# A list scheduler with other hand-over times and another choice, and some weight tiles placed 64 bytes in

## The chip, the cores and the metric

The kernel runs on one core of a Trainium2 chip. The metric is the device time of one launch in microseconds (us), the median over several runs.

## The reference

Three blocks follow one another: a retention (attention with decay and without softmax), a mixture of eight experts, and a feed-forward network with a squared ReLU.

```
def _attn_ref(q, k, v):                      # 8 x 8 heads, 576 positions, 64 wide
    scores = scale * np.matmul(q, k.transpose(0, 1, 3, 2))
    Dmat = np.where(rel >= 0, gamma[:, None, None] ** rel[None, :, :], 0.0)
    return np.matmul(scores * Dmat[None, :, :, :], v)

def _moe_ref(x, modality_id, w_gate, modality_bias, w1, w2):   # x: 4608 x 512, w1: 8 x 512 x 1024
    e_idx = np.argmax(x @ w_gate + modality_bias[modality_id], axis=1)
    ...
        h = np.maximum(x[mask] @ w1[e], 0.0)
        out[mask] = gate_w[mask, None] * (h @ w2[e])

def _moe2_ref(x, w_in, w_out):               # w_in: 512 x 2048, w_out: 2048 x 512
    h = np.maximum(x @ w_in, 0.0)
    return h * h @ w_out
```

All is float32. The kernel gets that accuracy from TensorE by splitting each operand into a high and a low part (type fp32r in the profile) and adding three products: high by high, high by low, low by high.

## The kernel before

The program has three stages, one after the other on every engine. Up to 182 us it computes the retention and the gate. Up to 609.7 us it runs the experts: tokens are sorted into slots (a first one called E, then 0 to 8), each of which is one tile of tokens for one expert. A slot is 512 tokens wide, but slots 6, 7 and 8 are narrow: 448, 384 and 256. In `first` and `second` (matmuls in lines 839 to 841) TensorE holds a 128 x 128 block of the expert's weights, `wx` or `wy`, and streams the tokens, `xh`/`xl` or `hh`/`hl`, past it. `wsplit` writes `wx` and `wy` (high and low parts) into buffers of the pool `wp`. Beside the experts this stage prepares the weights of the feed-forward network in memory (`wc`).

The rest, to the end, is the feed-forward network in `phase3`, on which most of the change bears. It is done by a scheme of seven products in place of eight for 2 x 2 blocks. The tokens are nine tiles of 512, and the hidden width is worked off in three passes of 3, 2 and 3 blocks (`q`), so there are 27 steps `n` of one pass and one tile; pass 1 takes the tiles in reverse. A **group** is six matmuls of TensorE, 128 x 256 each (lines 1211 to 1213). `one(n, q, x)` records one group for product x of the first layer, in the order x = 1, 2, 6, 5, 7, 4, 3, into a bank X, Y or Z, and what follows it: copies of a bank to a tile `z` by ScalarE (line 1186), additions by VectorE (line 1189, an operand from a bank), squares (`sq`: line 1197 on VectorE, or lines 1194 and 1195 on ScalarE), and the splits of `z` into the high part of `h` (ScalarE, line 1320) and the low part (VectorE, line 1321). `two(n, x)` records the groups of the second layer, one for each q, into a bank R, and the additions of the result to `oe` or, in every second tile, to the same place in `yr`. There are two banks for X, two for Y, one for Z, so a group waits until the copy or addition of an earlier product has read its bank.

In pass 0, `xprep` makes the seven operands of the next tile from the tokens in `yr`: eight additions in place and seven pairs of a copy (high part) and a subtraction (low part), into the tiles `x0` to `x3`; `xc` keeps them for the later passes, which load them. In the last pass the rows of a finished tile go out by four scatters, issued by GpSimd (line 1328).

`Plan` holds all that `phase3` records, with a duration for each entry. `emit` gives each entry a due time (its place in the recorded order of TensorE, less the durations and hand-overs behind it, with a `SLACK` for work on the other engines) and then places entries one at a time: those whose inputs are placed are candidates, each with the earliest start on its engine. The order so chosen is fixed; at run time engines only wait for one another's semaphores. So the numbers in `Plan` set nothing but the order of each engine's instructions, and for `sq` also the engine.

Of the kernel before, what the change touches and what calls it, by code (L numbers as in the profile page):

```python
# [10 lines left out]
F32R = mybir.dt.float32r  # L11
# [11 lines left out]
NT, DM = B * S, H * D  # L23
NE, FE = 8, 1024
FF = 2048
P = 128
NTILE = NT // P
TS = 512
# [4 lines left out]
KD = DM // P  # L33
# [59 lines left out]
def kernel(ctx, tc, qT, kT, kN, vN, modT, w_gate, mbias, w1, w2, w_in, w_out,  # L93
# [6 lines left out]
    wp = ctx.enter_context(tc.tile_pool(name="wp", bufs=10))  # L100
# [326 lines left out]
    def new(pool_, shape, dt, tag, name):  # L427
        return fixed[name] if name in fixed else pool_.tile(shape, dt, tag=tag, name=name)
# [15 lines left out]
    def expert(s):  # L444
        src = eslot[0:1, 0:1] if s == "E" else slots[0:1, 0, s:s + 1]
        ereg.clear()
        ereg[s] = sp.value_load(src, min_val=0, max_val=NE - 1)

    def wsplit(key, h, eng):
        if h == 0:  # L450
            x = new(wp, [P, 2, KD, 2 * P], F32R, "w", "wx")
            split(x[:, 0], x[:, 1], raws.pop((key, 0)), eng)
            W[key] = [x]
        else:
            y = new(wp, [P, 2, 2, DM], F32R, "w", "wy")
            split(y[:, 0], y[:, 1], raws.pop((key, 1)), eng)
            W[key].append(y)

# [2 lines left out]
    def width(s):  # L461
        return WIDE.get(s, TS)
# [252 lines left out]
    def phase12():  # L715
        ring[0] = psG
        with ExitStack() as c1:
# [258 lines left out]
            def extras():  # L976
                fixed.update({
                    "wr1": wr.tile([P, KD, 2 * P], F32, tag="wr", name="cwr1"),
                    "wr2": wr.tile([P, 2, DM], F32, tag="wr", name="cwr2"),
                    "wx": wp.tile([P, 2, KD, 2 * P], F32R, tag="w", name="cwx"),  # L980
                    "wy": wp.tile([P, 2, 2, DM], F32R, tag="w", name="cwy"),
                    "ix": ip.tile([P, 4], I32, tag="ix", name="cix"),
                    "xg": rp.tile([P, 4, DM], F32, tag="raw", name="cxg"),
                    "xh": xp.tile([P, KD, TS], F32R, tag="xh", name="cxh"),
                    "xl": xp.tile([P, KD, TS], F32R, tag="xl", name="cxl"),
                    "pst": psG.tile([P, 4, P], F32, tag="g", name="cpst"),
                    "psh": psG.tile([P, TS], F32, tag="g", name="cpsh"),
                    "hh": hp.tile([P, TS], F32R, tag="hh", name="chh"),
                    "hl": hp.tile([P, TS], F32R, tag="hl", name="chl"),
                })  # L990
                fixed["ye"] = fixed["xg"]
                fixed["y0"] = fixed["y2"] = tpb
                fixed["y1"] = fixed["y3"] = psG.tile([P, TS], F32, tag="g", name="cyb")
                extra(0)
                fixed.clear()
# [7 lines left out]
            for i, u in enumerate(us):  # L1003
                s, f = u
                k = seq.index(s)
# [83 lines left out]
    AT1 = {1: 0, 2: 1, 6: 3, 5: 5, 7: 6, 4: 9, 3: 11}  # L1089

    class Plan:
        HAND = 0.25
        SLACK = 6.0
        OVER = {"ACT": 0.14, "DVE": 0.11}

        def __init__(self):
            self.ops, self.wrote, self.read = [], {}, {}

        def add(self, engs, fn, r=(), w=(), land=0.0):
            deps = set()  # L1100
# [10 lines left out]
                self.wrote[k] = [i]  # L1111
                self.read[k] = []

        def emit(self, ahead=400, near=0.15):
            n = len(self.ops)
            lat = lambda i: min(t for _, t in self.ops[i][0])
            at, due = 0.0, [0.0] * n
            for i, (engs, _, _, _) in enumerate(self.ops):
                due[i] = at + (0.0 if engs[0][0].name == "PE" else self.SLACK)
                at += engs[0][1] if engs[0][0].name == "PE" else 0.0  # L1120
            for i in range(n - 1, -1, -1):
                engs, _, deps, _ = self.ops[i]
                for d in deps:
                    same = len(engs) == 1 and self.ops[d][0] and self.ops[d][0][0][0] is engs[0][0]
                    due[d] = min(due[d], due[i] - lat(d) - self.ops[d][3] - (0.0 if same else self.HAND))
            free, end, on, starts = {}, {}, {}, []
            todo = list(range(n))
            ready = {}
            while todo:
                cand = []  # L1130
                for i in todo[:ahead]:
                    engs, fn, deps, land = self.ops[i]
                    if i not in ready:
                        if any(d not in end for d in deps):
                            continue
                        ready[i] = [max([end[d] + (0 if on[d] == e.name else self.HAND) for d in deps],
                                        default=0.0) for e, _ in engs]
                    _, s0, e, t = min(((max(r_, free.get(e.name, 0.0)) + t, max(r_, free.get(e.name, 0.0)), e, t)
                                       for (e, t), r_ in zip(engs, ready[i])), key=lambda z: z[:2])
                    cand.append((s0, due[i], i, e, t))  # L1140
                first_ = min(c[0] for c in cand)
                lead = min((c for c in cand if c[0] == first_), key=lambda c: c[1:3])
                s0, _, i, e, t = min((c for c in cand if c[0] <= first_ + near and c[3] is lead[3]),
                                     key=lambda c: c[1:3])
                free[e.name] = s0 + t * (1.0 - self.OVER.get(e.name, 0.0))
                end[i] = s0 + t + self.ops[i][3]
                on[i] = e.name
                starts.append((s0, len(starts), i, e))
                todo.remove(i)
            for s0, _, i, e in sorted(starts, key=lambda z: z[:2]):  # L1150
                self.ops[i][1](e.h)
            self.starts = starts
# [5 lines left out]
    def phase3():  # L1158
        with ExitStack() as c2:
            ff = c2.enter_context(tc.tile_pool(name="ff", bufs=1))  # L1160
            sb = lambda name, shape, dt=F32R: ff.tile(shape, dt, tag=name, name=name)
            plan = Plan()
            for j in (1, 2):
                wload2(1, j, wp, False)
            WT = [[[held["w", m, j, x] for x in range(2)] for j in range(3)] for m in range(2)]
            XT = [held["x", m] for m in range(7)]
            HT = [sb(f"h{j}", [P, 2 * 7 * 256 + 128])[:, 56 + 32 * (j % 2):56 + 32 * (j % 2) + 2 * 7 * 256]
                  .rearrange("p (x m c) -> p x m c", x=2, m=7) for j in range(3)]
            ZT = [sb(f"z{j}", [P, 8, 256], F32) for j in range(3)]
            yr = rp.tile([P, KD, TS], F32, tag="raw", name="yr")  # L1170
# [7 lines left out]
            PE_, ACT_, DVE_, POOL_, DMA_ = (Eng(n_, h_) for n_, h_ in  # L1178
                                            (("PE", pe), ("ACT", act), ("DVE", dve), ("POOL", pool), ("DMA", sp)))
# [33 lines left out]
                        e.matmul(ps[n], ll, rh, start=False, stop=True, skip_group_check=True)  # L1213
                return go

            MMS = [(PE_, 0.72)]

            def loadw(p, m, j0=0):
                for j, fp in list(enumerate(PASSES[p]))[j0:]:
# [50 lines left out]
            def one(n, q, x):  # L1270
# [6 lines left out]
                kx, ky, kz = ("X", u % 2), ("Y", u % 2), ("Z",)  # L1277
                z, h = ZT[u % 3], HT[u % 3]
                kz_ = lambda *i: [("z", u % 3, j) for j in i]
# [52 lines left out]
            def two(n, x):  # L1332
# [4 lines left out]
                for q in range(len(PASSES[p])):  # L1337
                    u = HS_[n, q]
                    h, m, w, mo = HT[u % 3], MH[x], WT[1][q], MO[x]
                    plan.add(MMS, six([ps[:, 0, :], ps[:, 1, :]],  # L1340
                                      [((h[:, 0, m, P * b:P * b + P], h[:, 1, m, P * b:P * b + P]),
# [108 lines left out]
```

## Time and profile before

| | us |
|---|---|
| median of 3 runs (1332.58 to 1333.44) | 1332.95 |
| the profiled execution, its own time | 1330.45 |
| its span in the trace | 1328.7 |

The profiled execution's span lies 1.75 us inside its own time, and that time lies 2.5 us under the median. TensorE's granted clock is at its full level (1.00) in nearly all of the span. An engine can be called busy and still lose time: a matmul's end is modelled, so a wait is best read from the distance between the starts of two matmuls.

### The profile page before, as it was taken

The page shows a single profiled execution, that of the slowest core. Times are in us where ns is not written, and L with a number is a line of the kernel's source. Part 1 is how long each engine was busy: PE and PEld are TensorE (multiplying, and loading weights), DVE is VectorE, ACT ScalarE, POOL GpSimd, SP SyncE. Part 2 cuts the span into 40 slices and gives each one's busy share as a digit, 9 for nine tenths or more (in the row PEclk, how much of TensorE's full clock was granted, in tenths as well). Part 3 has the DMA queues.
Part 4 walks back from the last instruction along what each step waited for, and adds up shares of the span by engine and source line. Part 5 has one row for each costly group of instructions (what it writes and reads, how often), then busy time and mean ns, then how long its engine had stood idle before and what let it go on. Part 6 is the DMA issues. An engine that isn't in the chain of part 4 may idle for free.

```text
span 1328.7 us, 26978 instructions
## 1 busy us (share of the span) xinstructions
PE 1284.4 (97%) x10639; PEld 1196.3 (90%) x10639; DVE 1023.2 (77%) x2095; ACT 623.1 (47%) x1283; POOL 125.3 (9%) x170
## 2 busy tenths in 40 slices
PE   7999989999999999899999999999999999999996
PEld 6888877888888888899999999999999999999996
DVE  3877859878887887665888888867888777777665
ACT  2344444545445444454655556534344344443343
POOL 3222112101100110000000000000000011111121
PEclk9999999999999999899999999999999999999999
DMA  9998257787777877779555554678799866555451
GB/s 330 390 346 300 88 183 245 264 296 272 279 280 264 285 258 270 273 268 351 206 205 221 219 197 175 245 263 309 289 348 345 298 225 211 206 196 175 175 192 47
DMA packets 152499, 331.89 MB, mean 250 GB/s; under 512 B 15440, under 2 KB 67440, under 8 KB 152368
## 3 DMA queue, kind: packets, MB, share of 16 engines
q1 hardware_dynamic: 144752, 309.82, 65.5%
q0 software_dynamic: 5840, 19.14, 4.0%
q8 instruction: 85, 1.39, 0.4%
q10 hardware_dynamic: 1776, 1.17, 0.3%
q14 instruction: 46, 0.38, 0.1%
HBM read 222.33 MB, written 107.78 MB: 248 GB/s over the span
## 4 chain that ended last, share of the span: by engine, by line
PE 40%; DVE 12%; DMA 1%; issue 1%; ACT 0%; POOL 0%; POOLq 0%; DVEq 0%
PE bank L1213 13%; PE bank L1211 13%; PE bank L1212 13%; DVE z L1189 5%; DVE h L1321 3%; DVE z L1197 2%; DMA x<-xc 1%; DVE x L1189 1%; DVE yr L1189 1%; PE bank L839 0%; PE bank L840 0%; PE bank L841 0%; ACT h L1320 0%; DVE oe L1189 0%; POOL out L1328 0%
## 5 line engine op out<-in xcount | busy, mean ns | idle before, releaser
L1211 PE MATMUL bank<-x,w 128*128 128x256 f32 x1008 | 279.6, 277 | 7.5 <-ACT z L1186 5.4
L1212 PE MATMUL bank<-x,w 128*128 128x256 f32 x1008 | 279.4, 277 | 4.4 <-DVE x L1189 4.4
L1211 PE MATMUL bank<-w,h 128*128 128x256 f32 x1008 | 279.9, 278 | 2.6 <-DVE oe L1189 2.0
L1213 PE MATMUL bank<-w,h 128*128 128x256 f32 x1008 | 279.6, 277 | 0.7 <-DVE h L1321 0.7
L1213 PE MATMUL bank<-x,w 128*128 128x256 f32 x1008 | 278.6, 276 | 0.0
L1212 PE MATMUL bank<-w,h 128*128 128x256 f32 x1008 | 278.4, 276 | 0.0
L1186 ACT ACTIVATE z<-bank 128x256 f32<-128x256 f32 x288 | 108.4, 380 | 231.6 <-PE bank L1213 229.9
L1320 ACT ACTIVATE h<-z 128x512 fp32r<-128x512 f32 (+2 forms) x270 | 158.5, 600 | 89.8 <-DVE z L1189 71.1
L1211 PEld LDWEIGHTS bank<-x,w 128*128 128x128 f32 x1008 | 189.3, 188 | 9.4 <-ACT z L1186 6.9
L1212 PEld LDWEIGHTS bank<-x,w 128*128 128x128 f32 x1008 | 189.2, 188 | 6.0 <-DVE x L1189 6.0
L1211 PEld LDWEIGHTS bank<-w,h 128*128 128x128 f32 x1008 | 189.3, 188 | 3.9 <-DVE oe L1189 2.6
L1213 PEld LDWEIGHTS bank<-w,h 128*128 128x128 f32 x1008 | 189.2, 188 | 1.5 <-DVE h L1321 1.4
L1213 PEld LDWEIGHTS bank<-x,w 128*128 128x128 f32 x1008 | 189.3, 188 | 0.1
L1212 PEld LDWEIGHTS bank<-w,h 128*128 128x128 f32 x1008 | 189.3, 188 | 0.0
L1321 DVE TENSOR_TENSOR h<-z,h 128x512 fp32r<-128x512 f32 (+2 forms) x270 | 169.1, 649 | 7.6 <-ACT h L1320 7.6
L1189 DVE TENSOR_TENSOR z<-z,bank 128x256 f32<-128x256 f32 x216 | 89.4, 417 | 64.0 <-PE bank L1213 55.2
L839 PE MATMUL bank<-xh,wx 128*128 128x512 f32 (+3 forms) x320 | 119.5, 373 | 4.1 <-ACT xh L794 2.7
L839 PE MATMUL bank<-hh,wy 128*128 128x512 f32 (+3 forms) x320 | 122.7, 383 | 0.0
L840 PE MATMUL bank<-xl,wx 128*128 128x512 f32 (+3 forms) x320 | 119.2, 373 | 1.0 <-DVE xl L795 1.0
L840 PE MATMUL bank<-hl,wy 128*128 128x512 f32 (+3 forms) x320 | 119.8, 374 | 0.2 <-DVE hl L856 0.2
L841 PE MATMUL bank<-hh,wy 128*128 128x512 f32 (+3 forms) x320 | 119.7, 374 | 0.0
L841 PE MATMUL bank<-xh,wx 128*128 128x512 f32 (+3 forms) x320 | 119.1, 372 | 0.0
(185 smaller groups left out, 2131.0 us busy)
## 6 DMA issues: line engine op xcount, KB each, us to landing
x<-xc SPq DMA_DIRECT2D x112, 512.0 KB
wr<-w SPq DMA_DIRECT2D x80, 512.0 KB
xc<-x SPq DMA_DIRECT2D x63, 512.0 KB
wc<-cwh SPq DMA_DIRECT2D x16, 896.0 KB
wc<-cwl SPq DMA_DIRECT2D x16, 896.0 KB
w<-wc SPq DMA_DIRECT2D x16, 896.0 KB
pd<-oe SPq DMA_DIRECT2D x24, 512.0 KB
xd<-xs SPq DMA_DIRECT2D x9, 1024.0 KB
```

What stands on the lines that cost most here:

```text
L839: pe.matmul(ps, lh, rh, start=first, stop=False)
L840: pe.matmul(ps, lh, rl, start=False, stop=False)
L841: pe.matmul(ps, ll, rh, start=False, stop=last)
L1186: plan.add(a_(c), lambda e: e.activation(o, i, f), r, w)
L1189: plan.add(engs or d_(c), lambda e: e.tensor_tensor(out=o, in0=a, in1=b, op=op), r, w)
L1197: e.scalar_tensor_tensor(out=z, in0=z, scalar=0.0, in1=z, op0=ALU.max, op1=ALU.mult)
L1211: e.matmul(ps[n], lh, rh, start=first and n == 0, stop=False, skip_group_check=True)
L1212: e.matmul(ps[n], lh, rl, start=False, stop=False, skip_group_check=True)
L1213: e.matmul(ps[n], ll, rh, start=False, stop=True, skip_group_check=True)
L1320: plan.add(a_(c), lambda e: e.activation(h[:, 0, a:b], z[:, a + 1:b + 1], AF.Copy), rs, ks[0])
L1321: plan.add(d_(c), lambda e: e.tensor_tensor(out=h[:, 1, a:b], in0=z[:, a + 1:b + 1], in1=h[:, 0, a:b].bitcast(F32), op=ALU.subtract), rs + ...
```

## The change

Four things are edited. (1) In `Plan` one hand-over time between engines, 0.25, becomes three: from TensorE 0.20, to TensorE 0.10, between the others 0.05; a group is put at 0.685 in place of 0.72, `SLACK` is 10 in place of 6. (2) In `emit` the choice among the candidates: before, the engine of the earliest candidate was taken and on it, of those that could start within 0.15, the one that was due first; now simply the candidate that can start first, and of equals the one that is due first. (3) In `wsplit` (and the tiles that stand in for it in the extra slots, `cwx` and `cwy`) the buffers are 64 elements longer, and the weights of slots 6, 7 and 8 begin 16 elements, 64 bytes, in. (4) The tiles `HT` are 64 elements shorter and begin at 56, 24 and 56 elements, in place of 56, 88 and 56.

```
+    def place(key, t):
+        o = 0 if width(key[0]) == TS else 16
+        return t[:, o:o + 8 * 2 * P]
+
     def wsplit(key, h, eng):
         if h == 0:
-            x = new(wp, [P, 2, KD, 2 * P], F32R, "w", "wx")
+            x = place(key, new(wp, [P, 2 * KD * 2 * P + 64], F32R, "w", "wx")).rearrange(
+                "p (x k f) -> p x k f", x=2, k=KD)
...
     class Plan:
-        HAND = 0.25
-        SLACK = 6.0
+        FROM_PE, TO_PE, HAND = 0.20, 0.10, 0.05
+        SLACK = 10.0
...
+        def hand(self, a, b):
+            if a == b:
+                return 0.0
+            return self.TO_PE if b == "PE" else self.FROM_PE if a == "PE" else self.HAND
...
-                first_ = min(c[0] for c in cand)
-                lead = min((c for c in cand if c[0] == first_), key=lambda c: c[1:3])
-                s0, _, i, e, t = min((c for c in cand if c[0] <= first_ + near and c[3] is lead[3]),
-                                     key=lambda c: c[1:3])
+                s0, _, i, e, t = min(cand, key=lambda c: c[:3])
...
-            HT = [sb(f"h{j}", [P, 2 * 7 * 256 + 128])[:, 56 + 32 * (j % 2):56 + 32 * (j % 2) + 2 * 7 * 256]
+            HT = [sb(f"h{j}", [P, 2 * 7 * 256 + 64])[:, 56 - 32 * (j % 2):56 - 32 * (j % 2) + 2 * 7 * 256]
...
-            MMS = [(PE_, 0.72)]
+            MMS = [(PE_, 0.685)]
```

The lines of the changed kernel stand 9 higher from `Plan` on (line 1189 is 1198, 1320 is 1329).

What (1) and (2) move is seen in the orders of the engines. First VectorE in a tile of pass 0 (tile 5). `x2<-yr,x2` is the low half of the next tile's operand for product 6, `x1<-xt,x1` that for product 5; `z` with one number are additions and `L1197` squares, `L1321` the low halves of `h`. Before:

```order
L1189 TENSOR_TENSOR yr_10376<-yr_10376,xt_10377 128x2x256
L1189 TENSOR_TENSOR x0_5885<-yr_10376,x0_5885 128x512
L1197 SCALAR_TENSOR_TENSOR z2_10375<-z2_10375 128x256
L1321 TENSOR_TENSOR h2_10372<-z2_10375,h2_10372 128x256
L1321 TENSOR_TENSOR h1_10371<-z1_10374,h1_10371 128x512 x2
L1189 TENSOR_TENSOR z2_10375<-z2_10375 128x256
L1189 TENSOR_TENSOR yr_10376<-yr_10376 128x2x256 x2
L1189 TENSOR_TENSOR z2_10375<-z2_10375 128x256 x3
L1189 TENSOR_TENSOR x2_5887<-yr_10376,x2_5887 128x512
L1321 TENSOR_TENSOR h2_10372<-z2_10375,h2_10372 128x256
```

And of the change, at the same place:

```order
L1198 TENSOR_TENSOR xt_10377<-yr_10376 128x512
L1330 TENSOR_TENSOR h2_10372<-z2_10375,h2_10372 128x256
L1198 TENSOR_TENSOR x0_5885<-yr_10376,x0_5885 128x512
L1330 TENSOR_TENSOR h2_10372<-z2_10375,h2_10372 128x256
L1198 TENSOR_TENSOR z2_10375<-z2_10375 128x256 x2
L1198 TENSOR_TENSOR yr_10376<-yr_10376,xt_10377 128x2x256
L1198 TENSOR_TENSOR x0_5885<-yr_10376,x0_5885 128x512
L1330 TENSOR_TENSOR h1_10371<-z1_10374,h1_10371 128x512
L1198 TENSOR_TENSOR yr_10376<-yr_10376 128x2x256 x2
L1330 TENSOR_TENSOR h2_10372<-z2_10375,h2_10372 128x512
L1198 TENSOR_TENSOR x2_5887<-yr_10376,x2_5887 128x512
```

The subtraction into `xt`, which stood ahead of product 3's addition of block 0, has come down to this stretch, and three low halves of `h2`, two single and one double, that stood behind the low half of product 6 (the first of them is the last row of before) now stand ahead of it. On TensorE, in the same tile, 25 groups stood between product 3 of block 0 and product 6 of the next tile's block 0; now 30 stand there, because second-layer groups of the tile before, which ran behind the next tile's first groups, now run ahead of them.

Second, ScalarE in a tile of pass 2 (the last). `z1<-bank` and `z2<-bank` are copies that free a bank X for TensorE, `L1320` the high halves of `h`, and 1194 with 1195 a square. Before:

```order
L1186 ACTIVATE z1_10374<-bank6_90 128x256
L1320 ACTIVATE h0_10370<-z0_10373 128x512
L1186 ACTIVATE z2_10375<-bank5_89 128x256
L1194 ACTIVATE z1_10374<-z1_10374 128x256
L1195 ACTIVATE z1_10374<-z1_10374 128x256
L1320 ACTIVATE h0_10370<-z0_10373 128x512
L1186 ACTIVATE z1_10374<-bank6_90 128x256
L1186 ACTIVATE z2_10375<-bank5_89 128x256
L1186 ACTIVATE z1_10374<-z1_10374 128x256
L1320 ACTIVATE h1_10371<-z1_10374 128x768
L1186 ACTIVATE z2_10375<-bank5_89 128x256
```

And of the change:

```order
L1195 ACTIVATE z1_10374<-bank5_89 128x256
L1195 ACTIVATE z2_10375<-bank6_90 128x256
L1329 ACTIVATE h0_10370<-z0_10373 128x512
L1195 ACTIVATE z1_10374<-bank5_89 128x256
L1195 ACTIVATE z1_10374<-z1_10374 128x256
L1195 ACTIVATE z2_10375<-bank6_90 128x256
L1329 ACTIVATE h1_10371<-z1_10374 128x768
L1329 ACTIVATE h0_10370<-z0_10373 128x512
L1203 ACTIVATE z1_10374<-z1_10374 128x256
L1204 ACTIVATE z1_10374<-z1_10374 128x256
L1195 ACTIVATE z2_10375<-bank6_90 128x256 x2
```

The first copy `z2<-bank` has moved ahead of the first double high half of `h0`; one square on ScalarE (two instructions) has gone from this place, and the next copy `z2<-bank` now stands behind that high half, a copy and a square in one instruction; the third stands behind another high half and a square in two. TensorE's own order has not changed in this stretch.

## Rows read from the trace of the kernel before

**Rows 1.** The page's first part: busy time, share, instructions of each engine

```profile
PE 1284.4 (97%) x10639; PEld 1196.3 (90%) x10639; DVE 1023.2 (77%) x2095; ACT 623.1 (47%) x1283; POOL 125.3 (9%) x170
```

**Rows 2.** Windows, passes 0 and 2: PE, PEld, DVE, ACT, POOL busy, clock, DMA share

```profile
609.70:873.00 263.30, 258.86 (x2259) 257.12 (x2258) 223.92 (x481) 159.77 (x337) 0.10 (x1) 1.00 0.59 216
...
1041.00:1321.30 280.30, 271.63 (x2353) 268.49 (x2352) 205.80 (x439) 118.18 (x277) 35.88 (x66) 1.00 0.55 191
```

**Rows 3.** Waits of TensorE in passes 0, 1, 2: us in total, times, longest

```profile
PE bank L1212 <- DVE x L1189: 4.4, 8, 1.2
...
PE bank L1211 <- DMA x<-xc: 2.0, 1, 2.0
...
PE bank L1211 <- ACT z L1186: 5.4, 8, 0.7
PE bank L1211 <- DVE oe L1189: 2.0, 3, 0.8
PE bank L1213 <- DVE h L1321: 0.7, 1, 0.7
PE bank L1211 <- ACT h L1320: 0.6, 1, 0.6
```

**Rows 4.** Windows of one tile, in pass 0 and in pass 2

```profile
723.50:752.70 29.20, 28.85 (x252) 28.66 (x252) 25.70 (x56) 17.82 (x39) 0.00 (x0) 1.00 0.53 199
...
1240.60:1270.18 29.58, 28.90 (x253) 28.70 (x253) 21.61 (x48) 12.73 (x31) 4.34 (x8) 1.00 0.57 195
```

**Rows 5.** Timeline of TensorE at a tile boundary of pass 0: start, us, instruction

```profile
752.08 0.28 PE L1211 MATMUL bank<-x,w 128*128 128x256 f32 x1
752.70 0.39 PE L1212 MATMUL bank<-x,w 128*128 128x256 f32 x1 [0.35 <-DVE x L1189]
752.92 0.28 PE L1213 MATMUL bank<-x,w 128*128 128x256 f32 x1
```

**Rows 6.** Timeline of VectorE, pass 0: product 3's addition, product 6's low half

```profile
765.16 0.42 DVE L1189 TENSOR_TENSOR z<-z,bank 128x256 f32<-128x256 f32 x1
...
781.16 0.68 DVE L1189 TENSOR_TENSOR x<-yr,x 128x512 fp32r<-128x512 f32 x1
```

**Rows 7.** Timeline of a tile in pass 2, TensorE, VectorE and ScalarE

```profile
1265.82 0.28 PE L1213 MATMUL bank<-x,w 128*128 128x256 f32 x1
...
1267.18 0.28 PE L1213 MATMUL bank<-x,w 128*128 128x256 f32 x1
...
1267.38 0.42 DVE L1189 TENSOR_TENSOR z<-z,bank 128x256 f32<-128x256 f32 x1 [2.34 <-PE bank L1213]
...
1267.51 0.39 ACT L1186 ACTIVATE z<-bank 128x256 f32<-128x256 f32 x1 [0.90 <-PE bank L1213]
...
1269.22 0.63 ACT L1320 ACTIVATE h<-z 128x512 fp32r<-128x512 f32 x1 [1.32 <-DVE z L1189]
...
1269.76 0.37 ACT L1186 ACTIVATE z<-bank 128x256 f32<-128x256 f32 x1
...
1270.18 0.38 PE L1211 MATMUL bank<-x,w 128*128 128x256 f32 x1 [0.68 <-ACT z L1186]
```

**Rows 8.** Timeline of TensorE, the first and the twelfth 448-wide matmul of one row

```profile
500.27 0.36 PE L839 MATMUL bank<-xh,wx 128*128 128x448 f32 x1
...
502.49 0.37 PE L841 MATMUL bank<-xh,wx 128*128 128x448 f32 x1
```

**Rows 9.** Timeline of TensorE, the first and twelfth 384-wide matmul of one row

```profile
569.80 0.33 PE L839 MATMUL bank<-xh,wx 128*128 128x384 f32 x1
...
571.71 0.34 PE L841 MATMUL bank<-xh,wx 128*128 128x384 f32 x1
```

**Rows 10.** Timeline of TensorE, slot 8: the branch's wait, 256-wide matmuls

```profile
593.80 0.39 PE L839 MATMUL bank<-xh,wx 128*128 128x256 f32 x1 [1.37 <-DVEq L958]
...
594.50 0.28 PE L841 MATMUL bank<-xh,wx 128*128 128x256 f32 x1
...
595.71 0.28 PE L839 MATMUL bank<-hh,wy 128*128 128x256 f32 x1
```

More of the change, by code (lines that the diff above doesn't have):

```diff
@@ L454, in wsplit @@
         else:
-            y = new(wp, [P, 2, 2, DM], F32R, "w", "wy")
+            y = place(key, new(wp, [P, 2 * 2 * DM + 64], F32R, "w", "wy")).rearrange(
+                "p (x k f) -> p x k f", x=2, k=2)
             split(y[:, 0], y[:, 1], raws.pop((key, 1)), eng)
@@ L979, in extras @@
                     "wr2": wr.tile([P, 2, DM], F32, tag="wr", name="cwr2"),
-                    "wx": wp.tile([P, 2, KD, 2 * P], F32R, tag="w", name="cwx"),
-                    "wy": wp.tile([P, 2, 2, DM], F32R, tag="w", name="cwy"),
+                    "wx": wp.tile([P, 2 * KD * 2 * P + 64], F32R, tag="w", name="cwx"),
+                    "wy": wp.tile([P, 2 * 2 * DM + 64], F32R, tag="w", name="cwy"),
                     "ix": ip.tile([P, 4], I32, tag="ix", name="cix"),
@@ L1112, in add, with emit @@
                 self.read[k] = []
-        def emit(self, ahead=400, near=0.15):
+        def emit(self, ahead=400):
             n = len(self.ops)
@@ L1124, in emit @@
                     same = len(engs) == 1 and self.ops[d][0] and self.ops[d][0][0][0] is engs[0][0]
-                    due[d] = min(due[d], due[i] - lat(d) - self.ops[d][3] - (0.0 if same else self.HAND))
+                    due[d] = min(due[d], due[i] - lat(d) - self.ops[d][3]
+                                 - (0.0 if same else self.hand(self.ops[d][0][0][0].name, engs[0][0].name)))
             free, end, on, starts = {}, {}, {}, []
@@ L1135, in emit @@
                             continue
-                        ready[i] = [max([end[d] + (0 if on[d] == e.name else self.HAND) for d in deps],
-                                        default=0.0) for e, _ in engs]
+                        ready[i] = [max([end[d] + self.hand(on[d], e.name) for d in deps], default=0.0)
+                                    for e, _ in engs]
                     _, s0, e, t = min(((max(r_, free.get(e.name, 0.0)) + t, max(r_, free.get(e.name, 0.0)), e, t)
```

## Prediction

> **What bounds the kernel now.** I read the page's first part first: TensorE is busy in 97% of the span, the next engine in 77% [rows 1]. So only time that TensorE loses can be won. The windows by stage come next [rows 2]: the feed-forward stage, the only one whose order the change touches, runs from 609.70 to 1321.30, 711.6 us. To see what it would take without a wait, take a boundary of two tiles in pass 0 [rows 5]. Matmuls start 0.113 us apart; here 0.62 lie between 752.08 and 752.70, which loses 0.51, and the second matmul after the pause comes 0.22 behind the first, which loses 0.11 more: 0.62 for a wait that the profile puts at 0.35. The tile's window is 29.20 us [rows 4]; without the 0.62 it is 28.58 for 252 matmuls, 0.1134 each. The stage has 24 x 252 = 6048 of them (nine tiles of 252, nine of 168, nine of 252): 685.9 us. **So 25.7 us are lost, and that is the most that a new order could give.** The list of waits by pass [rows 3] says where: in pass 0 eight waits for the low half of an operand (4.4 us by the profile; six like the one above, the first two 1.15 each by what is left); at the turn to pass 1 one wait of 2.0 for an operand's load; in pass 2 eight waits for ScalarE's copy of a bank, three for additions to `oe`, two for halves of `h`.
>
> **Pass 0.** TensorE reaches product 6 of the next tile before VectorE has written its low half. VectorE's stretch runs from product 3's addition (765.16) to that low half (781.16), 16.0 us [rows 6]; it starts when its group ends. Before, 25 groups stood between them, 25 x 0.68 = 17.0 us of TensorE; in the change 30, which is 20.4. On VectorE's side the stretch grows as the order's rows show: the subtraction into `xt` enters it (a 512-wide one, 0.60 behind the next as I read such pitches, 0.69 long at most, the low half's row being 0.68), three low halves of `h2` enter (two 256-wide, one 512-wide), and one square leaves to ScalarE; I make it 18.3. The low half has to be done some 0.9 before the matmuls (its own 0.68, and the hand-over): 18.3 + 0.7 = 19.0 against 20.4 less the hand-over from TensorE at the front and to it behind, 19.5. Half a microsecond is left, so the wait goes at seven of the eight boundaries: six times 0.62, and once 1.15 + 0.27 = 1.42 (the same surcharge as above), 5.1 together. The first boundary keeps its wait; the first tile's order has no such room. Bounds: 0, if VectorE comes 1.1 later than I count, and 5.1. I take 5.1, since every step has a row of its shape.
>
> **The turns and pass 1.** At the turn to pass 1 TensorE waits 2.0 (2.27 with the surcharge) for a load that was issued behind the new pass's weights. The change keeps the order of the loads and puts two more groups ahead of the waiting one: 2 x 0.68 = 1.36, so 1.3; bounds 0.5 (the load may start later) and 1.4. At the turn to pass 2 two waits for halves of `h` (0.6 and 0.7, with surcharges 2.1 in all); two groups move in between one of them, I take 0.9, bounds 0 and 1.5. Pass 1 has no row of waits for VectorE or ScalarE, but six of its tiles each lose about 0.2 in short restarts; I take 0.8 of 1.2, bounds 0 and 1.2. Together 3.0.
>
> **Pass 2.** Here is the largest loss, 29.58 - 28.58 = 1.0 per tile in eight tiles [rows 4], and I expect the change to move it, not to remove it. The rows show its cause [rows 7]. TensorE's last matmul of product 3, block 0, starts at 1265.82; VectorE's addition starts at 1267.38, 1.56 later. Elsewhere a reader of a bank starts about 0.33 after the last matmul (1267.18 to ScalarE's copy at 1267.51 in the same rows). So VectorE's start is some 1.25 late, with nothing in the views that holds it; I have not explained it. It makes the high half of `h0` late (1269.22), behind it stands the copy of a bank (1269.76), and TensorE waits 0.68 for that copy (0.95 with what lies around it). The change moves the copy ahead of the high half, so this wait goes. But the next copy of a bank X now stands behind the high half, a copy and a square: 0.54 from the high half to what follows (1269.22 to 1269.76) and two instructions of about 0.37. And VectorE now does a 768-wide low half and another addition between product 3's square and the sums that the high half needs, which makes that 1 us later still. Counted from product 3's group, the high half starts at 4.9, the copy at 4.9 + 0.5 + 0.7 = 6.2 and is done at 6.6, where TensorE wants its bank at 6.1: 0.5 and 0.1 for the restart. The copy behind it, after another high half and a square in two, costs 0.2 and 0.1. That is 0.92 for 0.95. I take 0.2 us for the eight tiles. If VectorE's late start doesn't recur, all copies are in time and the term is 8 x 0.95 = 7.6; that is the upper bound, and the lower is 8 x (0.95 - 1.25) = -2.4, should the copy be held by another hand-over as late. In the last tile the additions to `oe` keep two of their three waits; one of 0.7 goes.
>
> **The weights 64 bytes in.** A 256-wide matmul of slot 8 comes every 0.121 us (594.50 to 595.71, ten steps) [rows 10], in the feed-forward stage every 0.1134. By columns, 0.443 ns each, a 448-wide one should take 0.1984 and takes 2.22/11 = 0.2018 [rows 8]; a 384-wide one 0.1701, and takes 1.91/11 = 0.1736 [rows 9]. Each narrow slot has 192 matmuls: 192 x (0.0034 + 0.0035 + 0.0076) = 2.8 us is the upper bound. What is different in the two places no view tells; addresses are one candidate, the order of the three products another. The lower bound is 0: they may have nothing to do with it, or a wait ahead takes what is won, as at the branch before slot 8, where TensorE waits 1.37 [rows 10]. I take 1.5: most of slot 8 lies behind that wait, of the others I count half.
>
> The Trainium skill has a rule against this term: SBUF — State Buffer, "Who interferes with whom", gives TensorE two independent read ports, one for the moving operand and one for loading weights, and says that PE and ACT never wait on anyone. By it an address changes nothing, the term is 0 and the sum 1324.0. The two paces at full clock show that something does slow the slots' matmuls; whether it is the address, no run here shows yet.
>
> **The `HT` tiles** move by 256 bytes or not at all (24 and 88 elements differ by 256 bytes, each tile is 256 bytes shorter), and the longer weight buffers push those behind them by 256 bytes each. No instruction is added or removed. I count 0: the stage's matmuls run at 0.1134 whichever tile they read, so there is no excess to win. What a worse place would cost is bounded by the slots' excess, 0.0034 to 0.0076 on a third of the 3024 matmuls that read `h`, 3.4 to 7.7 us; nothing in the views speaks for it.
>
> **The sum.** 5.1 + 3.0 + 0.2 + 0.7 + 1.5 = 10.5. The profiled execution's own time is 1330.45, which gives 1320.0; the median lies 2.5 higher, so **1322.5**.
>
> **The rivals.** (B) VectorE's late start in pass 2 is bound to the order around it and goes: 7.4 more, 1315. For it: no other pass shows it. Against it: TensorE's order and the scatters at that place are unchanged. (C) Pass 0 keeps its waits, because VectorE's stretch there is 0.5 longer than I count and then some: 5.1 less, 1327.5. For it: VectorE is busy 223.9 of 263.3 us there, and the room is thin. Against: the square that leaves, and pauses of VectorE in the same stretch. (D) The new order gives with one hand and takes with the other: no change, 1333. (E) It ends slower: a late start like that of pass 2 comes on the path elsewhere too. A choice that always takes the earliest start fills VectorE with work that is not urgent; then one hand-over 1.25 late in each tile of pass 1 and a second in each of pass 2 cost 18 x 1.25 = 22.5, less the 10.5, 1345. It decides from about nine such (10.5/1.25 = 8.4). For it: ScalarE's copies in pass 2 now stand behind squares and high halves. Against: pass 0 and pass 1 of before, with a fuller VectorE, show none.
>
> **How the numbers follow.** The forecast has 0.55, with its own range 1319 to 1326 from the bounds of the smaller terms; B 0.12, C 0.15, D 0.08, E 0.10. The runs of before lie within 0.86 us, so 0.2% (2.7 us) is about what can be told from no change. Faster is the forecast, B and C, 0.82; same is D, 0.08; slower is E, 0.10. The range, 1313 to 1330, takes in the forecast, B and C with their margins, and leaves out D and E.
>
> **What the profile will show.** In pass 0 tiles of 28.6 in windows, and no wait of product 6 for a low half but the first. At the turn a wait of about 0.9 in place of 2.27. In pass 2 tiles still of 29.5, with waits at the copies of X for block 2's products 7 and 4 in place of product 6's; if they are 28.6, it was B. In slot 8 matmuls 0.113 apart. The forecast is wrong if VectorE's stretch in pass 0 passes 19.5 us, if pass 2's late start goes or spreads, or if pass 1 shows new waits.

## The result and the profile after

The changed kernel takes 1320.31 us (median of 6 runs, 1319.58 to 1323.54), the kernel before 1332.76 beside it (6 runs): a ratio of 0.9904, 95% interval 0.9894 to 0.9915. That is 12.4 us faster; the sum had 10.5. Here and below a median is of all runs of a kernel, while a ratio leaves out runs far slower than the rest, so it is not exactly the quotient of the two medians. The profiled execution takes 1319.88 with a span of 1318.1, 10.6 under the one of before (1330.45).

The page's first part says as little as before [rows 1]: TensorE is still at 97%, since what it lost and what the span lost are the same time.

```profile
PE 1278.9 (97%) x10639; PEld 1192.3 (90%) x10639; DVE 1009.5 (77%) x2075; ACT 630.3 (48%) x1323; POOL 125.6 (10%) x170
```

Where the time went is read from windows that begin with a pass's first matmul and end with the next pass's first, or with the last matmul of all (window, length, TensorE's busy time and matmuls, clock, DMA share, GB/s). A pass needs 2268, 1512 and 2268 matmuls at 0.1134 us: 257.2, 171.5 and 257.2. Before:

```profile
609.74:874.32 264.58, 260.14 (x2271) 1.00 0.59 215
874.32:1053.06 178.74, 175.35 (x1515) 1.00 0.88 321
1053.06:1321.00 267.94, 260.58 (x2270) 1.00 0.54 184
```

After:

```profile
608.25:866.60 258.35, 257.91 (x2270) 1.00 0.61 222
866.60:1040.83 174.23, 173.52 (x1514) 1.00 0.89 324
1040.83:1310.26 269.43, 260.72 (x2269) 1.00 0.54 186
```

The stage starts 1.5 us earlier, pass 0 is 6.2 shorter, pass 1 with its turns 4.5, and pass 2 is 1.5 **longer**: 10.7 in all. The lists of TensorE's waits say the same (pass 0; pass 1, where the one wait lies behind the turn to it; from the turn to pass 2 on), against [rows 3]: of eight waits for low halves one is left, the wait for a load is gone, and the eight waits for ScalarE have grown from 5.4 to 7.2.

```profile
PE bank L1221 <- DVE x L1198: 0.3, 1, 0.3
...
PE bank L1222 <- DVE h L1330: 0.3, 1, 0.3
...
PE bank L1220 <- ACT z L1195: 7.2, 8, 1.1
PE bank L1220 <- DVE oe L1198: 1.8, 3, 0.8
```

In pass 0, VectorE's stretch from product 3's addition to product 6's low half is now 18.2 us (timeline of VectorE), and TensorE comes to that product without a pause (timeline of TensorE; the matmul ahead of it starts at 778.77):

```profile
759.36 0.42 DVE L1198 TENSOR_TENSOR z<-z,bank 128x256 f32<-128x256 f32 x1 [0.88 <-PE bank L1222]
...
777.58 0.69 DVE L1198 TENSOR_TENSOR x<-yr,x 128x512 fp32r<-128x512 f32 x1
...
778.88 0.28 PE L1220 MATMUL bank<-x,w 128*128 128x256 f32 x1
```

The low half is done at 778.27, 0.61 ahead of the product's first matmul. (The 25 and 30 groups counted before take in product 3's own: by TensorE's order 24 stood between that group and product 6, and now 29. The 29 take 19.7 us, of which 19.5 are left from VectorE's start at 759.36 to 778.88.) What pass 2 waits for is seen in a tile's timeline:

```profile
1134.36 0.28 PE L1222 MATMUL bank<-x,w 128*128 128x256 f32 x1
...
1134.67 0.39 ACT L1195 ACTIVATE z<-bank 128x256 f32<-128x256 f32 x1 [0.97 <-PE bank L1222]
1135.04 0.28 PE L1222 MATMUL bank<-x,w 128*128 128x256 f32 x1
...
1135.39 0.97 POOL L1337 DMA_INDIRECT out<-oe,ix  x1 [0.19 <-issue]
1135.72 0.28 PE L1222 MATMUL bank<-x,w 128*128 128x256 f32 x1
...
1137.34 0.38 ACT L1195 ACTIVATE z<-bank 128x256 f32<-128x256 f32 x1 [1.83 <-PE bank L1222]
1137.42 0.42 DVE L1198 TENSOR_TENSOR z<-z,bank 128x256 f32<-128x256 f32 x1 [2.48 <-PE bank L1222]
...
1137.78 0.38 PE L1220 MATMUL bank<-x,w 128*128 128x256 f32 x1 [1.10 <-ACT z L1195]
```

The group whose last matmul starts at 1134.36 is read by ScalarE 0.31 after that start. The next one, product 6 of block 1, has its last matmul at 1135.04 and is read 2.30 later; product 3 of block 0 has it at 1135.72 and VectorE reads it 1.70 later, at nearly the same moment. ScalarE had nothing else to do: the engine was idle for 1.83. What lies there is the tile's fourth scatter (1135.39). In the kernel before it is the same: the fourth scatter starts 0.33 ahead of product 3's last matmul [rows 7], but only product 3 was struck.

```profile
1265.49 0.97 POOL L1328 DMA_INDIRECT out<-oe,ix  x1 [0.19 <-issue]
```

So both kernels have a stretch of some 2 us beside the fourth scatter in which finished groups of TensorE are seen late. In the changed kernel that strikes a copy that frees a bank X, and TensorE stands for 1.10.

The trace's record of semaphore updates says on which side the delay lies. Elsewhere in this stage TensorE's update is recorded 0.29 after a group's last matmul starts; for the two groups here it is recorded 2.28 and 1.67 after, and the readers start within 0.03 of it. So it is the update that is late, and not the reader. GpSimd's own update beside the scatter comes on time. Some of ScalarE's have no record there, so whether the hold is TensorE's alone is not shown. By the same record 8 groups come late in before, one in each of eight tiles, and 15 in the changed kernel.

### The profile page after: what moved, and what is told of

It is laid out like the page before. It is cut to its first block, busy times and chain, and to the rows that moved or that the text cites. A ratio compares the mean times of both kernels' runs of the same rounds, so it can differ in the third digit from the quotient of the medians.

```text
span 1318.1 us, 27015 instructions
## 1 busy us (share of the span) xinstructions
PE 1278.9 (97%) x10639; PEld 1192.3 (90%) x10639; DVE 1009.5 (77%) x2075; ACT 630.3 (48%) x1323; POOL 125.6 (10%) x170
## 4 chain that ended last, share of the span: by engine, by line
PE 50%; DVE 3%; DMA 0%; ACT 0%; POOL 0%; issue 0%; POOLq 0%; DVEq 0%
PE bank L1222 17%; PE bank L1220 16%; PE bank L1221 16%; DVE z L1198 1%; DVE h L1330 1%; DMA x<-xc 0%; PE bank L845 0%; PE bank L847 0%; PE bank L846 0%; DVE z L1206 0%; DVE oe L1198 0%; ACT z L1195 0%; POOL out L1337 0%; ACT h L1329 0%; POOLq L1455 0%
## 5 line engine op out<-in xcount | busy, mean ns | idle before, releaser
L1329 ACT ACTIVATE h<-z 128x512 fp32r<-128x512 f32 (+2 forms) x270 | 152.2, 596 | 42.2 <-DVE z L1198 40.0
```

The costliest lines, as they stand in the source:

```text
L1329: plan.add(a_(c), lambda e: e.activation(h[:, 0, a:b], z[:, a + 1:b + 1], AF.Copy), rs, ks[0])
```

## The experiments

Runs 1 to 4 shared one chip, 5 to 8 another, 9 to 11 a third, run 12 had a fourth, and before ran beside them: it took 1334.0, 1325.5, 1333.4 and 1323.9 us. That turned out to matter.

**1 and 2: the numbers alone, the choice alone.**

```
# run 1: the new numbers and HT, the weights at 0 as in run 3, and in emit the old choice:
+                first_ = min(c[0] for c in cand)
+                lead = min((c for c in cand if c[0] == first_), key=lambda c: c[1:3])
...
# run 2: the kernel before with
+                s0, _, i, e, t = min(cand, key=lambda c: c[:3])
```

> The kernel of before with the new numbers of the planner (hand-overs 0.20, 0.10 and 0.05, slack 10, a group at 0.685) and the new HT tiles, but with the old choice among candidates and the weights of the narrow slots at the start of their buffers. Theory 1 (the numbers make the gain): on TensorE 30 groups stand between product 3 of block 0 and the next tile's product 6 in pass 0, as in the changed kernel, so the waits of pass 0 go; the feed-forward stage takes 703 us or less from its first to its last matmul (before 711.3, after 702.0), the run 1323 to 1327 us. Theory 2 (the choice makes it): waits for low halves stay in pass 0, about 4 us, and the run is at 1329 to 1333.

> The kernel of before with only the new choice among candidates (earliest start, then due time); numbers, HT and weights as before. Theory 1 (the numbers make the gain): 25 groups stand in pass 0 where the changed kernel has 30, so product 6 still waits there, six times 0.35 us or more; the run is at 1329 to 1335 us. Theory 2 (the choice makes it): pass 0 loses under 2 us and the run is at 1323 to 1327.

Measured: 1329.01 with the numbers (ratio 0.9966, interval 0.9954 to 0.9977), 1322.33 with the choice (0.9912, 0.9894 to 0.9930). The passes with the numbers, then with the choice:

```profile
609.00:870.66 261.66, 261.00 (x2271) 1.00 0.60 218
870.66:1049.19 178.53, 177.98 (x1514) 1.00 0.86 318
1049.19:1317.51 268.32, 261.17 (x2269) 1.00 0.54 185
```

```profile
610.70:870.93 260.23, 258.49 (x2271) 1.00 0.61 222
870.93:1045.39 174.46, 173.32 (x1515) 1.00 0.89 327
1045.39:1315.52 270.13, 261.82 (x2270) 1.00 0.53 183
```

Their waits of pass 0, by the lists as above:

```profile
PE bank L1224 <- DVE x L1201: 0.5, 1, 0.5
...
PE bank L1209 <- DVE x L1186: 1.0, 1, 1.0
```

Neither theory held whole. With the numbers the waits of pass 0 go, as theory 1 said, but the time is theory 2's. With the choice they go as well, against theory 1, and the time is 0.7 under theory 2's; pass 0 still loses 3.0 where theory 2 had under 2. Pass 0 gains with either (2.9 and 4.4 of 6.2), and pass 1 gains with the choice alone (4.3 of 4.5). In run 1, 29 groups stand ahead of product 6 as in the changed kernel, and VectorE's stretch is 19.1 us (762.13 to 781.19). With the choice the six waits of 0.35 go although only 24 groups stand there, as in before, because VectorE's stretch has become shorter, 15.0 us in place of 16.0 [rows 6]:

```profile
763.69 0.42 DVE L1186 TENSOR_TENSOR z<-z,bank 128x256 f32<-128x256 f32 x1
...
778.73 0.68 DVE L1186 TENSOR_TENSOR x<-yr,x 128x512 fp32r<-128x512 f32 x1
```

So there are two ways to win the same wait, more groups of TensorE ahead or less of VectorE; the parts do not add up.

**3 and 8: the weights' place.**

```
     def place(key, t):
-        o = 0 if width(key[0]) == TS else 16
+        o = 0                                   # run 3
+        o = 0 if width(key[0]) == TS else 32    # run 8
```

> The changed kernel with the weights of the narrow slots at the start of their buffers, as before; the buffers keep their 64 additional elements. If the place is the cause of the slots' slower matmuls: slot 8's 256-wide matmuls come 0.120 us apart in place of 0.113, and the run is 1.0 to 1.6 us slower than the changed kernel (ratio 1.0008 to 1.0012), 1321.3 to 1322.0. If the place does nothing: 0.113 apart and the same time within 0.3 us.

> The changed kernel with the weights of the narrow slots 128 bytes into their buffers in place of 64; read from the profile alone, by the pace of the matmuls. If any distance from the buffer's start serves: 256-wide matmuls 0.1135 us apart, as with 64 bytes. If the place counts by its remainder to 128 bytes: 0.120 apart, as with 0 bytes, and the feed-forward stage starts 1.2 us later than in the changed kernel.

Slot 8's matmuls by the timeline of TensorE, the first and the last of an unbroken row: of the changed kernel (64 bytes, 13 steps in 1.47 us, 0.113), of run 3 (0 bytes, 13 in 1.56, 0.120), of run 8 (128 bytes, 15 in 1.78, 0.119).

```profile
594.20 0.28 PE L847 MATMUL bank<-xh,wx 128*128 128x256 f32 x1
...
595.67 0.28 PE L845 MATMUL bank<-hh,wy 128*128 128x256 f32 x1
```

```profile
594.16 0.28 PE L846 MATMUL bank<-xl,wx 128*128 128x256 f32 x1
...
595.72 0.28 PE L847 MATMUL bank<-hh,wy 128*128 128x256 f32 x1
```

```profile
595.45 0.28 PE L847 MATMUL bank<-xh,wx 128*128 128x256 f32 x1
...
597.23 0.28 PE L847 MATMUL bank<-hh,wy 128*128 128x256 f32 x1
```

So the place sets slot 8's pace in these three, and 64 bytes serve where 128 hardly do. It is not the whole cause: run 7, which has 64 bytes too, has 0.114 ahead of the branch (585.17 to 589.49, 38 steps) and 0.118 behind it (593.74 to 596.10, 20 steps), and no view tells why. The place is worth 192 x (1.56 - 1.47)/13 = 1.3 us. In run 3 the feed-forward stage starts at 609.51 in place of 608.25, but one start says little: with 64 bytes the seven profiles have 607.1 to 609.9, mean 608.4, and with 0 the six have 609.0 to 610.7, mean 609.8. The means differ by 1.4, which fits. In the run's time that can't be told: 1320.91 (6 runs, 1318.70 to 1322.39), and its interval against before, 0.9885 to 0.9915, overlaps the changed kernel's.

**4: the fourth scatter later.** The scatter is recorded after the next tile's product 3 of block 2, and a copy out of that tile's `z` in place of the memset ahead of it makes GpSimd wait. Orders of the other engines stay.

```
-                e.memset(gap, 0.0)
+                if after is None:
+                    e.memset(gap, 0.0)
+                else:
+                    e.tensor_copy(gap, after)      # after: z_[:, 4, 0:1] of the next tile's block 2
...
                         for j in (j0, j0 + 1):
+                            if j == 1 and n + 1 < len(T3):
+                                held_back.append((n, oe, kk))
+                                continue
```

> The changed kernel with the fourth scatter of each tile in the last pass held back by about 13 us: the memset ahead of it becomes a copy of one column of the next tile's z (block 2, sum 4). In both kernels TensorE's finished groups are seen late by ScalarE and VectorE from the start of a tile's fourth scatter until 1.9 us after it, and not beside the first three. Theory 1 (the fourth scatter holds TensorE's signals): the late signals move with it by 13 us, to a stretch in which few copies are urgent; the waits of 1.1 us at copies of X in pass 2 go, pass 2 loses 3 us in place of 12.9, and the run is at 1309 to 1313. Theory 2 (something else at that place of the program holds them): product 6's copy of block 1 is still 2 us late beside the third scatter, pass 2 loses 11 to 13 us, and the run is at 1319 to 1322. Theory 3 (the last of a row of scatters does it, whichever it is): the late signals stay beside the third scatter and come a second time with the fourth, 1319 to 1325.

Measured: 1309.85 (1309.32 to 1311.09; ratio 0.9823, 0.9806 to 0.9841). Pass 2's window, and its waits, all in the last tile:

```profile
1040.71:1299.87 259.16, 257.60 (x2270) 1.00 0.56 194
```

```profile
PE bank L1220 <- DVE oe L1198: 1.6, 2, 0.8
```

10.3 us are back: the late signals go from where the fourth scatter was. Theory 1 holds in that, and theory 3 in part: beside the third scatter, now the last of its row, product 6's group (1132.39) is read 0.84 later in place of 0.31. That costs nothing here. They don't come a second time: beside the fourth scatter, which now stands alone, no update is late. Scatters first, then TensorE and ScalarE of the same tile:

```profile
1128.91 0.97 POOL L1342 DMA_INDIRECT out<-oe,ix  x1 [11.15 <-DVE oe L1198]
...
1130.19 0.97 POOL L1342 DMA_INDIRECT out<-oe,ix  x1 [0.19 <-issue]
...
1131.47 0.98 POOL L1342 DMA_INDIRECT out<-oe,ix  x1 [0.19 <-issue]
```

```profile
1132.39 0.28 PE L1222 MATMUL bank<-x,w 128*128 128x256 f32 x1
...
1133.23 0.39 ACT L1195 ACTIVATE z<-bank 128x256 f32<-128x256 f32 x1 [0.36 <-PE bank L1222]
```

**5, 6 and 7: two and two, before with the late scatter, wider spacing.**

```
+                            if j < 2 and n + 1 < len(T3):            # run 5, in place of j == 1
...
# run 6: the edit of run 4 on the kernel before
...
-                e.memset(gap, 0.0)                                   # run 7, on the changed kernel
+                for _ in range(6):
+                    e.memset(gap, 0.0)
```

> As the late fourth scatter, but the third and the fourth of each tile are held back together, so that scatters come in two rows of two. With the fourth alone held back, product 6's copy was still seen 0.5 us late beside the third. Theory 1 (a hold comes with the third scatter in a row, a longer one with the fourth): no finished group is seen late, pass 2 loses under 3 us, 1309 to 1311 us. Theory 2 (the last of a row holds the signals, whatever the row's length): late signals beside the second scatter of each row, of 0.5 us or more; if they strike a copy of X, pass 2 loses 4 to 12.

> The kernel of before with the fourth scatter of each tile in the last pass held back by about 13 us, and nothing else; the orders of TensorE, VectorE and ScalarE are those of before. If the fourth scatter's hold was the cause of pass 2's waits before: the eight waits of 0.68 at copies of X go, pass 2 loses 3 to 5 us in place of 11.4, and the run is 6.5 to 8 us faster than before, 1325 to 1327. If before waited for its own order of ScalarE (the copy behind the high half of h0) and the hold only added to it: at least half of the wait stays, 1328 to 1331.

> The changed kernel with six memsets ahead of each scatter in the last pass in place of one, so that scatters of a row come about 1.5 us later each, 2.5 to 3 us apart in place of 1.28. Theory 1 (a backlog: four scatters 1.28 apart are more than is drained, and the hold is the backlog's): with the wider spacing no signal is late, pass 2 loses under 4 us, 1310 to 1312 us. Theory 2 (the fourth scatter holds signals, whatever the spacing): a hold of 1.9 us from the fourth's start, now 4 to 5 us later in the tile; the run is at 1312 to 1322, by what it strikes.

Measured beside a before of 1325.54: 1309.27 (ratio 0.9885), 1324.07 (0.9997, 0.9983 to 1.0011), 1314.09 (0.9925; the wider spacing also delays the last tile's scatters, with nothing beside them). None of them tells what it was made for, because in the four traces from this chip no signal is late. Run 8, on the same chip, has the four scatters in a row as the changed kernel has them, and product 6 (last matmul 1134.65) is read 0.38 later, product 3 (1135.33) 0.31 later, beside the fourth scatter:

```profile
1134.65 0.28 PE L1222 MATMUL bank<-x,w 128*128 128x256 f32 x1
...
1134.99 0.97 POOL L1337 DMA_INDIRECT out<-oe,ix  x1 [0.19 <-issue]
1135.03 0.36 ACT L1195 ACTIVATE z<-bank 128x256 f32<-128x256 f32 x1
...
1135.33 0.28 PE L1222 MATMUL bank<-x,w 128*128 128x256 f32 x1
1135.64 0.42 DVE L1198 TENSOR_TENSOR z<-z,bank 128x256 f32<-128x256 f32 x1 [1.09 <-PE bank L1222]
```

Its pass 2 has no wait but the last tile's, and it took 1311.67 (one run):

```profile
1042.96:1302.05 259.09, 257.53 (x2270) 1.00 0.55 193
```

**9 and 10: the changed kernel, and before with the late scatter, again.** No edit beyond those shown.

> The changed kernel itself, beside before, on the chip of these runs. On the chip of the last runs the kernel of before took 1325.5 us in place of 1333 and a trace with four scatters in a row showed no late signals at all. If the late signals belong to the chip: on a chip where before takes 1333, TensorE loses about 12.9 us in pass 2 and the run is 12 to 13 us faster than before; on one where before takes 1325 to 1326, pass 2 loses 2.6, no group is seen late, and the run is at 1310 to 1312, 14 to 15 us faster than before. If they come and go with the execution: neither pair holds.

> The kernel of before with only the fourth scatter held back, beside before on the same chip. Where before takes 1333 (late signals): 6.5 to 8 us faster than before, 1325 to 1327. Where before takes 1325 to 1326 (no late signals): no difference, within 1 us.

This call's before took 1333.42. The changed kernel: 1321.11 (0.9902, 0.9872 to 0.9933). Before with the late scatter: 1322.75 (0.9914, 0.9892 to 0.9936), 10.7 us faster than before with this one edit, where 6.5 to 8 were expected. Pass 2 of the changed kernel, then of before with the late scatter and its waits:

```profile
1043.85:1312.57 268.72, 260.73 (x2270) 1.00 0.53 187
```

```profile
1054.85:1314.38 259.53, 257.81 (x2269) 1.00 0.55 189
```

```profile
PE bank L1211 <- DVE oe L1189: 1.7, 3, 0.8
```

The eight waits at copies of X are gone from before too, with ScalarE's order as it was. So they were the late signals' alone: 267.94 - 259.53 = 8.4 us in before, 10.3 in the changed kernel. (The medians differ by more than the 8.4, and why stays open; the profiled executions, 1323.86 and 1330.45, by 6.6, since pass 1 was slower in this one, 180.27, and the stage began 0.4 later.)

**11: two and two, and the last tile in another order.**

```
-                for x in (1, 2, 5, 6, 7, 4, 3):
+                for x in (1, 2, 5, 6, 7, 4, 3) if n + 1 < len(T3) else (1, 5, 6, 2, 7, 3, 4):
                     two(n, x)
...
-                if x in (2, 3, 7):
-                    y = {2: 1, 3: 6, 7: 7}[x]
+                end = n + 1 == len(T3)
+                if x in ((2, 3, 5) if end else (2, 3, 7)):
+                    y = {2: 1, 3: 6, 5: 7, 7: 7}[x]
```

> The changed kernel with two scatters of each tile held back, and in the last tile the second layer's products in the order 1, 5, 6, 2, 7, 3, 4 with the addition of product 5 to its quarter taken right after it, so that groups of product 3 stand between products 6 and 7 while VectorE reads the bank. One of the last tile's two waits of 0.78 (1.06 with what lies around it) goes: 1308 to 1309 us on either kind of chip, 1.0 us below the kernel with two scatters held back. If VectorE's additions are late by themselves: both waits stay, 1309 to 1310.

Measured on the chip of runs 9 and 10: 1308.63 (1306.32 to 1309.88; ratio 0.9806, 0.9786 to 0.9825), the fastest version, 24.8 us under before. In its profile no group is read late beside either scatter of a row of two: the group whose last matmul starts 0.84 behind the second scatter is read 0.38 later, where in run 4 the one 0.92 behind the third was read 0.84 later.

```profile
1132.28 0.97 POOL L1342 DMA_INDIRECT out<-oe,ix  x1 [0.19 <-issue]
...
1133.12 0.28 PE L1222 MATMUL bank<-x,w 128*128 128x256 f32 x1
...
1133.50 0.42 DVE L1198 TENSOR_TENSOR z<-z,bank 128x256 f32<-128x256 f32 x1 [0.74 <-PE bank L1222]
```

That answers run 5's question on a chip that has late signals, for its theory 1. One of the last tile's waits is gone, and pass 2 is 1.0 us shorter than in run 4:

```profile
PE bank L1220 <- DVE oe L1198: 0.8, 1, 0.8
```

```profile
1042.79:1300.94 258.15, 257.37 (x2269) 1.00 0.55 195
```

**12: wider spacing again.** As run 7, but the last tile as in the changed kernel.

> The changed kernel with the scatters of a row 2 to 2.5 us apart in place of 1.28 (six memsets ahead of each, in all tiles but the last), beside before. It tells something only where before takes 1333, that is, where late signals occur. Theory 1 (a backlog): no group is seen late, pass 2 loses under 4 us, 1310 to 1312 us. Theory 2 (the third and fourth scatter in a tile hold signals, whatever the spacing): late signals beside the third and the fourth, now 2 to 4 us later in the tile, and the run at 1312 to 1321. Where before takes 1325 to 1326: 1310 to 1312, and nothing told.

Before took 1323.9 here: 1310.74 (0.9909, 0.9891 to 0.9927). No signal is late in its trace, but before's time suggests that none would have been late with the old spacing either, so nothing is told of the spacing. In run 7 the last tile's wider spacing had cost 3 us: from TensorE's last matmul to the end of the span there are 10.9 us, here 7.8. And it shows something else: with the changed kernel's orders on such a chip the gain is 13.2 us, about what it is on the others (12.4), as is to be expected if both kernels are rid of the late signals there.

## Why the prediction came out as it did

**Pass 0 (5.1 forecast, 6.2 measured).** Right in its mechanism: VectorE's stretch 18.2 for 18.3, the margin 0.61 for 0.5, all waits gone but the first boundary's, and TensorE's room the 19.5 us that were taken, though from a count that is one group too high. The size was off at that boundary: I let its wait of 1.2 stand, and it fell to 0.3. Runs 1 and 2 add what I had not seen: the shorter stretch of VectorE alone would have done it.

**The turns and pass 1 (3.0 forecast, 4.5 measured).** Right in sign and too low in size, and not at the first turn. There I took 0.9 of the wait for the load to remain. It went whole, but shorter waits came there, 1.4 in all (the largest for a low half of `h`, 0.3 by the list). By the distances between starts of matmuls that turn gained 1.2 where I had 1.3. What is above the forecast came from pass 1's short restarts (1.4 for 0.8) and from the turn to pass 2 (1.5 for 0.9); 0.4 are spread over the pass. The gain comes from the choice among candidates (run 2), not from the numbers (run 1: 178.53, where before had 178.74).

**Pass 2 (0.2 and 0.7 forecast, -1.5 measured).** The step that failed is the one that I left unexplained: "VectorE's start is some 1.25 late, with nothing in the views that holds it". I took it for something that befalls VectorE's addition, and built a queue on ScalarE from there. It befalls every update of TensorE that falls due in some 2 us beside the fourth scatter, so its price depends on which groups end in that stretch. In before it struck product 3, of which ScalarE's queue made 0.95 a tile; in the changed kernel it strikes product 6's copy of block 1 too, and TensorE waits already at product 7 of that block, not at products 7 and 4 of block 2 as I had said. Six of eight tiles wait about 1.1 by the profile there, the other two 0.3, where I had a wait of 0.5 and one of 0.2; a tile takes 29.96 (1137.78 to 1167.74) where I had 29.5. The lower bound of the term, -2.4, had been set for another hand-over as late; that is what came, -2.2 in the eight tiles. The copies behind high halves and squares, on which I put the price, are in time when the hold is gone (run 4). In the last tile one of three waits for `oe` went, as forecast (the list after has three, but one of 0.2 is at the turn). Rival B did not occur: the late start was not bound to the order, and it stayed and spread. Against B I had named the scatters as unchanged, and they were the cause. Where the hold is absent the changed orders take 1310.7 (run 12) and 1311.7 (run 8), but before is faster there too, so that is not B's gain.

**The weights (1.5 forecast, 1.3 measured).** Right in sum, not in its parts: slot 8 gives nearly all of it. A 448-wide matmul takes 0.203 after (eleven steps from 500.12 to 502.35) and a 384-wide one 0.175 (eleven from 569.25 to 571.17), no less than before [rows 8, 9]; over all steps of the slot the 448-wide ones gain 0.3 us at most. So the half that I counted for those slots was wrong, and slot 8's own excess was worth more than I took. The Trainium skill (SBUF — State Buffer, "Who interferes with whom") says that PE never waits on anyone. It speaks there of engines that contend with one another; that a place changes nothing I had read into it. Slot 8 does not bear that reading out, with 0.120, 0.113 and 0.119 at 0, 64 and 128 bytes, and the measurement decides.

**The sum.** 10.5 forecast, 10.6 between the two profiled executions, 12.4 between medians: it held because pass 0 and the turns gave 2.6 more and pass 2 gave 2.4 less than forecast, and that these cancel is luck. Of the 2.2 us by which the median lies under the 1322.5, 2.1 are the distance from the profiled execution to the median, taken as 2.5 and here 0.4. E, the slower rival, did not occur, though its mechanism did: late signals in more places than before. The changed kernel had one more in most tiles of pass 2, none in pass 1. HT's new places were not tried by themselves; run 1, which has them, shows no pass longer than before by more than 0.4.

## What to carry to other kernels

A wait whose cause no view names should not be taken as a constant: before its price is forecast it should be moved, by shifting its neighbours one at a time; here one held-back scatter was worth 10.3 us, nearly as much as the whole change. In a list scheduler the wait of TensorE for another engine can be won from either side, so parts of a change that win the same wait don't add up. Where a time differs between chips by more than between runs, an experiment can tell only where the effect shows, and before has to run beside it.

## What the hardware showed that I had not expected

Beside the fourth of four scatters 1.28 us apart, groups that TensorE had finished were read up to 2.3 us later in place of 0.31, beside the third of three 0.84; beside rows of two not at all. TensorE itself went on meanwhile. This occurred in the traces of before and after and on the two chips of the experiments where before took 1333 to 1334. It did not on one where before took 1325.5: there the same scatters at the same distances left the readers at 0.31 to 0.38 (run 8). On the chip where before took 1323.9 only the wider spacing was traced, so there it is before's time that speaks for it. Each chip's runs were made at one time, so chip and occasion are not told apart. What in the scatters holds the signals, and what differs, stays open: the spacing was tried twice, both times where before shows no hold.

The pace of 256-wide matmuls depends on where the weights lie: 0.113 us with 64 bytes ahead of them, 0.120 with none, 0.119 with 128, at a granted clock of 1.00. One trace with 64 bytes, run 7, has 0.118 in part of the slot, which stays unexplained.
